# Products with zeros moved between three places in an attention and soft-MoE kernel

## The chip, the cores and the metric

The kernel runs on one core of a Trainium2 chip. The metric is device time in microseconds of one execution; several executions are taken and their median is compared. TensorE is called PE, VectorE DVE, ScalarE ACT, GpSimd POOL, and SyncE, which issues the stores, SP.

## The reference

The first part is attention over 4 batches, 8 heads, 768 positions and head size 64. Some heads see all earlier positions, the others only 4 first positions and a window of 64. The second part is a soft mixture of experts over the 3072 rows of the result (512 columns): 8 experts with 4 slots each.

```
scores = where(mask, q @ k.T / 8, -1e9);  a = softmax(scores);  x = a @ v      # as 3072 x 512
logits = x @ phi                                  # 3072 x 32
slot_input = softmax(logits, over rows).T @ x     # 32 x 512
h = relu(slot_input[e] @ w1[e]);  slot_out[e] = h @ w2[e]      # each expert e, w1 512x1024, w2 1024x512
out = softmax(logits, over slots) @ slot_out      # 3072 x 512
```

## The kernel before, in words

The work is a list of named operations. A planner (`Plan.run`) places them by keys, costs and free buffers, and so fixes one order; the program is then emitted in this order, and each engine works through its own queue.

Attention goes in sixteen groups, `p` from 0 to 15 (batch times pair of heads). In each, PE forms scores (L641) into a score bank (`scb`, two of them, two halves each), ACT takes exponentials (L713), DVE masks them (L658), PE multiplies them with the values into `pvb` (L773), DVE normalizes (L787), PE transposes the result (`XT.p`, L799) and DVE copies it (`XE.p`).

At the end of each batch come the products with phi (`LG.b`, L814), their exponentials (`EL.b`, L829, on ACT), the slots' sums (`DS.b`, L844), their addition on DVE (`SA.b`, L862 for the last batch) and a transpose of the exponentials (`TE.b`, L872). `LG.3` and `DS.3` are those of the last batch. Then `SI` (L929) folds the four partial sums with four small products, and a copy gives `siT`.

The experts follow. `H.e4.c` (L945) is the first layer for four experts at a time and one half of the hidden columns, 16 products each; ACT applies the ReLU, `TH` (L967) transposes, DVE copies. `W2.e` (L990) is the second layer of expert `e`, eight products into `pvb[:, 0, :]`. The last expert comes in two parts: `W2.7` gives columns 0 to 255, `W2.8` the rest. Between `W2.5` and `W2.6` stands `RW` (L1027), 24 products for the rows' sums. ACT scales the first half of the slots' output (`SOa`, L1004) after `W2.7` and the second half (`SOb`) after `W2.8`.

The output is formed from 30 products `OM.gi.r.d0` (L1056): six over columns 0 to 255 ahead of `W2.8`, six over columns 256 to 511, and 18 over all 512. `OM.0.0.0` is the first. ACT and DVE scale each into the output tile (L1064, L1066), and SP stores it in eleven pieces (L1083).

All weights come by DMAs issued by POOL (L283) in one fixed order; those of the last expert come last, in two pieces for `W2.7` and `W2.8`.

Apart from the work there are products of a tile of zeros (`zeros_for`, L1155 to L1158), whose results nobody reads. The dictionary `before` maps an operation's name to how many of them stand ahead of it and in which bank they write. One loop fills it from the planned order: in the first 22 us of the plan, and from the last product of attention to the last expert wherever the plan leaves PE a gap of 0.6 us or more, at most three each (none ahead of `W2`). After that loop, some entries are set by hand (L1150 to L1153), and these lines are what the change touches. The last loop emits the zeros and then the operation.

Of the kernel before, what the change touches and what calls it, by code (L numbers as in the profile page):

```python
# [173 lines left out]
def kernel(  # L174
# [19 lines left out]
    NE, DM, F = moe_w1.shape  # L194
# [52 lines left out]
    scb = [ps.tile([P, 2, 512], F32, name=f"sc{i}") for i in range(2)]  # L247
    trb = [ps.tile([P, 512], F32, name=f"tr{i}") for i in range(2)]
    pvb = ps.tile([P, 2, 512], F32, name="pv")
# [773 lines left out]
    cs = Buf("SC")  # L1023
# [83 lines left out]
    before, free, shift, hist = {}, 1.2, 0.0, []  # L1107
# [39 lines left out]
        before[o.name] = (min(max(0, int(us / (w / 2400))), 0 if o.name[:2] == "W2" else 3), 0, bank, c0)  # L1147


    for k in ("XT.15", "LG.3", "DS.3"):  # L1150
        del before[k]
    before[f"W2.{NE - 1}"] = (8, 0, pvb[:, 1, :], 0)
    before["OM.0.0.0"] = (2, 0, pvb[:, 1, :], 0)  # L1153

    def zeros_for(n, m, bank, c0):  # L1155
        for w in [512 - c0] * n + [128] * m:
# [43 lines left out]
```

## Time and profile before

| | |
|---|---|
| median of 3 runs | 150.12 us (148.64 to 151.61) |
| the profiled execution | 149.16 us, its span 147.4 us |
| PE busy | 124.9 us, 85% of the span |
| DVE busy | 111.5 us, 76% |
| ACT busy | 109.7 us, 74% |
| mean granted clock of PE | 0.961 |
| DMA | 33.03 MB, mean 224 GB/s |

Times in the profile are microseconds from the first instruction. Lines such as L990 are lines of the kernel. A row of the timeline has the start, the time from the first start to the last end, the engine, the line, what is written from what, and the count; in brackets stands the idle time of the engine before it and what ended that. Durations of PE's products overlap, since they are pipelined. A row of stretches has the stretch, its length, the busy time and number of instructions of PE, its weight loads, DVE, ACT and POOL, then the clock granted to PE (1.00 is full), the busy share of the DMA engines and the GB/s that they moved.

### The profile page before, as it was taken

To read this page: it belongs to the slowest core of one execution; us is meant where nothing else is said; L and a number is where in the kernel's file an instruction comes from. 1 tells how busy PE (TensorE), PEld (TensorE's weight loads), DVE (VectorE), ACT (ScalarE), POOL (GpSimd) and SP (SyncE) were. 2 spreads that over 40 slices of the span, in tenths; PEclk is the share of its full clock that TensorE was granted. 3 is DMA by queue.
4 is the path that set the end of the run, shared out by engine and by line. 5 is a ranking of instruction groups with operands and counts; after the bars stand their busy time and mean duration, and the time that the engine had idled before them with its cause. 6 is when DMAs were issued, how large, how long until landed. Compare 5 with 4: busy or idle time off the path is not lost.

```text
span 147.4 us, 4968 instructions
## 1 busy us (share of the span) xinstructions
PE 124.9 (85%) x2169; PEld 80.3 (54%) x2169; DVE 111.5 (76%) x244; ACT 109.7 (74%) x143; POOL 24.0 (16%) x48
## 2 busy tenths in 40 slices
PE   6989999989899998999999999998748999789000
PEld 2355566668576675877576775765633457332000
DVE  3889299987999899899999999999848330179100
ACT  3374899989999999999998999999712620399200
POOL 6921111320111121101400111010700000100000
PEclk9999999999999999999999999999997899999955
DMA  4999999999999999999999999999999999879995
GB/s 97 186 213 217 223 210 210 213 212 226 213 209 210 215 222 216 218 218 197 214 217 229 216 213 213 216 216 213 213 218 218 213 213 188 117 240 389 409 422 249
DMA packets 9608, 33.03 MB, mean 224 GB/s; under 512 B 867, under 2 KB 4595, under 8 KB 7283
## 3 DMA queue, kind: packets, MB, share of 16 engines
q0 software_dynamic: 6912, 26.09, 88.5%
q1 hardware_dynamic: 2672, 6.62, 11.7%
q8 instruction: 17, 0.28, 0.7%
q14 instruction: 5, 0.04, 0.1%
q10 hardware_dynamic: 2, 0.00, 0.0%
HBM read 52.49 MB, written 6.29 MB: 399 GB/s over the span
## 4 chain that ended last, share of the span: by engine, by line
PE 34%; DVE 18%; DMA 17%; ACT 16%; issue 4%; POOL 4%; ACTq 1%; POOLq 0%
DMA slot<-in_v_dram 17%; ACT pt L713 9%; PE pv L773 8%; PE sc L641 6%; DVE pt L658 4%; DVE xv L787 4%; POOL slot L283 3%; ACT slot L1064 3%; PE tr L611 3%; PE pv L990 2%; PE tr L799 2%; DVE xT L278 2%; PE sc L945 2%; DVE qk L278 2%; PE tr L945 2%
## 5 line engine op out<-in xcount | busy, mean ns | idle before, releaser
L713 ACT ACTIVATE pt<-sc 128x1024 bf16<-128x1024 f32 x80 | 76.7, 1045 | 2.9 <-PE sc L641 2.5
L641 PE MATMUL sc<-qk 64*128 64x512 bf16 (+3 forms) x256 | 31.3, 308 | 2.6 <-ACT pt L713 1.8
L658 DVE TENSOR_TENSOR pt<-pt,msk 128x1024 bf16<-128x1024 bf16 (+1 forms) x48 | 29.9, 639 | 0.5 <-ACT pt L713 0.4
L773 PEld LDWEIGHTS <-pt 128*128 128x128 bf16 x640 | 23.4, 97 | 6.7 <-issue 5.6
L773 PE MATMUL pv<-vx,pt 128*128 128x65 bf16 x352 | 26.1, 193 | 0.1
L773 PE MATMUL pv<-vf,pt 128*128 128x65 bf16 x288 | 20.9, 194 | 0.0
L641 PEld LDWEIGHTS <-qk 64*128 64x128 bf16 x256 | 10.2, 93 | 11.6 <-issue 4.7
L611 PE MATMUL tr<-ident,slot 128*64 128x128 bf16 (+1 forms) x448 | 15.5, 219 | 0.5 <-DMA slot<-in_v_dram 0.5
L787 DVE TENSOR_TENSOR xv<-pv,rs 128x768 bf16<-128x768 f32 x16 | 15.3, 958 | 0.6
L611 PEld LDWEIGHTS <-slot 128*64 128x64 bf16 (+1 forms) x448 | 12.7, 110 | 3.6 <-issue 3.2
L283 POOL DMA_DIRECT2D slot<-in_moe_w_dram x15 | 8.1, 543 | 38.6 <-PE tr L611 10.0
L278 DVE COPY qk<-tr 128x768 bf16<-128x768 bf16 (+2 forms) x24 | 12.9, 551 | 1.0 <-PE tr L569 0.6
L278 DVE COPY xv<-tr 128x768 bf16<-128x768 bf16 (+2 forms) x20 | 8.4, 431 | 2.6 <-PE tr L569 2.6
L799 PE MATMUL tr<-ident,xv 128*128 128x128 bf16 x96 | 8.1, 220 | 2.2 <-DVE xv L787 1.9
L1157 PE MATMUL pv<-zero 128*128 128x512 bf16 x33 | 8.3, 380 | 0.6 <-ACT msk L1004 0.6
L278 DVE COPY xT<-tr 128x768 bf16<-128x768 bf16 x14 | 7.7, 554 | 1.0 <-PE tr L799 0.8
L799 PEld LDWEIGHTS <-xv 128*128 128x128 bf16 x96 | 5.7, 97 | 4.7 <-DVE xv L787 2.3
L676 PE MATMUL tr<-ident,xv 128*128 128x128 bf16 x96 | 7.9, 220 | 0.1
L278 DVE COPY vx<-tr 128x768 bf16<-128x768 bf16 x14 | 7.7, 550 | 0.2 <-PE tr L676 0.2
L692 DVE TENSOR_TENSOR vf<-vx,fm 128x528 bf16<-128x528 bf16 x16 | 6.9, 430 | 0.3
L676 PEld LDWEIGHTS <-xv 128*128 128x128 bf16 x96 | 5.7, 97 | 2.4 <-issue 1.7
L1004 ACT ACTIVATE msk<-pv,rcs 128x256 bf16<-128x256 f32 x2 | 0.9, 474 | 8.0 <-PE pv L990 8.0
(121 smaller groups left out, 166.5 us busy)
## 6 DMA issues: line engine op xcount, KB each, us to landing
slot<-in_moe_w_dram POOLq DMA_DIRECT2D x9, 1024.0 KB, 22.4
out_dram<-slot SPq DMA_DIRECT2D x4, 1024.0 KB, 7.1
slot<-in_q_dram POOLq DMA_DIRECT2D x3, 768.0 KB, 19.8
slot<-in_k_dram POOLq DMA_DIRECT2D x3, 768.0 KB, 14.4
slot<-in_moe_w_dram POOLq DMA_DIRECT2D x2, 896.0 KB, 22.7
slot<-in_v_dram POOLq DMA_DIRECT2D x2, 768.0 KB, 12.7
out_dram<-slot SPq DMA_DIRECT2D x6, 256.0 KB, 2.7
slot<-in_v_dram POOLq DMA_DIRECT2D x2, 512.0 KB, 24.6
```

The costliest lines, as they stand in the source:

```text
L278: nc.vector.tensor_copy(dst, src)
L283: emit=lambda o: nc.gpsimd.dma_start(dst(), src))
L611: nc.tensor.transpose(t[64 * i:64 * (i + 1), :, s, :], rv[:, i, 8 * c + s, :], ident[0:nr, 0:nr])
L641: nc.tensor.matmul(scb[sc.slot][:, i, c:c + 128 * nb], kk, qq.rearrange("p b c -> p (b c)"), start=True, stop=True)
L658: nc.vector.tensor_tensor(pw, pw, mw, op=ALU.mult)
L676: nc.tensor.transpose(t[:, 128 * j:128 * (j + 1)], vT[:, 6 * n + j, :], ident)
L692: nc.vector.tensor_tensor(vfs[VFb[p].slot], vv, fm[:, n], op=ALU.mult)
L713: nc.scalar.activation(pTs[PTb[b, n].slot][:, :, 512 * g:512 * (g + 1)], scb[sc.slot], ACT.Exp, scale=scale)
L773: nc.tensor.matmul(pvb[:, h, 65 * i:65 * (i + 1)], lt, rhs, start=(j == 0), stop=(j == i))
L787: nc.vector.tensor_tensor(xo, pvw[:, :, :, 0:64], r.rearrange("p i (j o) -> p i j o", o=1).to_broadcast([P, 2, 6, 64]), op=ALU.mult)
L799: nc.tensor.transpose(t[:, 128 * i:128 * (i + 1)], xv[:, i, 128 * n:128 * (n + 1)], ident)
L1157: nc.tensor.matmul(bank[:, c0:c0 + w], zero[:, 0:128], zero[:, 0:w], start=(c0 == 0), stop=True, skip_group_check=True)
```

## The change

The hand-set entries of `before` differ. Ahead of `OM.0.0.0` there were two products of zeros and are none. Ahead of `W2.7` there were eight and are seven. Ahead of `LG.3` there were none and are two; ahead of `DS.3` there were none, and now the number that the loop worked out stands again; ahead of `SI` there were none and is one, in the half score bank that `RW` does not use. `XT.15` has none, as before. Nothing else is changed, and the planned order of the other operations is the same.

```
-    for k in ("XT.15", "LG.3", "DS.3"):
-        del before[k]
-    before[f"W2.{NE - 1}"] = (8, 0, pvb[:, 1, :], 0)
-    before["OM.0.0.0"] = (2, 0, pvb[:, 1, :], 0)
+    before["LG.3"] = (2, *before["LG.3"][1:])
+    before["SI"] = (1, 0, scb[1 - cs.slot][:, 1, :], 0)
+    del before["XT.15"]
+    before[f"W2.{NE - 1}"] = (7, 0, pvb[:, 1, :], 0)
```

## The prediction

> **What bounds the kernel now.** I read the clock by stretches first, then the order of TensorE's work from the end of attention on, then when the weights land, then the DMA share while the outputs are stored.
>
> Mean granted clock and busy time by stretches of 3.41 us (columns: us, busy time and count of each engine, clock, DMA share, GB/s):
>
> ```profile
> 108.69:112.10 3.41, 1.80 (x25) 0.88 (x22) 1.41 (x3) 1.67 (x3) 0.00 (x0) 1.00 1.05 221
> 112.10:115.51 3.41, 3.22 (x32) 1.24 (x36) 3.39 (x2) 0.69 (x1) 0.00 (x0) 0.50 1.01 211
> 115.51:118.93 3.42, 3.27 (x52) 1.87 (x44) 0.84 (x2) 2.74 (x11) 0.00 (x0) 1.00 1.05 220
> 125.75:129.17 3.42, 2.61 (x24) 1.19 (x26) 0.84 (x2) 1.42 (x4) 0.40 (x1) 1.00 0.73 101
> 129.17:132.58 3.41, 2.71 (x21) 1.28 (x18) 2.61 (x7) 3.05 (x7) 0.00 (x0) 1.00 0.77 252
> 135.99:139.41 3.42, 0.26 (x2) 0.00 (x0) 1.02 (x2) 1.35 (x3) 0.00 (x0) 1.00 1.01 414
> 139.41:142.82 3.41, 0.00 (x0) 0.00 (x0) 0.00 (x0) 0.00 (x0) 0.00 (x0) 0.50 1.01 420
> ```
>
> The clock is halved in 112.10 to 115.51, just after the stretch in which PE was busy for only 1.80 us, and again from 139.41, eight such stretches later, just after one with 0.26 us. So I read it as a grid: a thin stretch is followed by a halved one. Stretches with 2.61 and 2.71 us kept the clock. The dividing line lies between 1.80 and 2.61 us, in this trace's measure.
>
> The order of the work around the change (start, duration, engine; in brackets the idle time before):
>
> ```profile
> 108.31 0.51 PE L799 MATMUL tr<-ident,xv 128*128 128x128 bf16 x6 [0.88 <-DVE xv L787]
> 109.47 0.31 PE L814 MATMUL tr<-phi,xT 128*128 128x32 bf16 x6 [0.65 <-DVE xT L278]
> 110.20 0.61 PE L844 MATMUL tr<-xv,elg 128*32 128x512 bf16 x6 [0.42 <-ACT elg L829]
> 111.60 0.30 PE L929 MATMUL tr<-sum,msk 128*128 128x32 bf16 x4 [0.34 <-DVE msk L862]
> 112.29 1.90 PE L945 MATMUL sc<-slot,msk 128*32 128x512 bf16 x16 [0.38 <-DVE msk L278]
> 113.97 2.67 PE L945 MATMUL tr<-slot,msk 128*32 128x512 bf16 x32
> 119.00 1.48 PE L990 MATMUL pv<-slot,xT 128*32 128x512 bf16 x24
> 120.31 0.60 PE L990 MATMUL pv<-qk,xT 128*32 128x512 bf16 x8
> 124.12 0.62 PE L990 MATMUL pv<-pt,xT 128*32 128x512 bf16 x8
> 124.67 1.90 PE L1157 MATMUL pv<-zero 128*128 128x512 bf16 x8
> 126.50 0.40 PE L990 MATMUL pv<-qk,xT 128*32 128x256 bf16 x8
> 127.48 0.59 PE L1157 MATMUL pv<-zero 128*128 128x512 bf16 x2 [0.58 <-ACT msk L1004]
> 127.91 0.27 PE L1056 MATMUL sc<-msk,expT 128*128 128x256 bf16 x1
> 128.74 0.27 PE L1056 MATMUL sc<-msk,expT 128*128 128x256 bf16 x1 [0.23 <-ACT slot L1064]
> 129.06 0.40 PE L990 MATMUL pv<-qk,xT 128*32 128x256 bf16 x8
> 130.04 0.27 PE L1056 MATMUL sc<-msk,expT 128*128 128x256 bf16 x1 [0.58 <-ACT msk L1004]
> ```
>
> L799, L814, L844 and L929 are XT.15, LG.3, DS.3 and SI; L945 is the experts' first layer (H), L990 the second (W2): 124.12 is W2.6, 126.50 is W2.7, 129.06 is W2.8. PE looks like the bound of this stretch. But W2.6, W2.7 and W2.8 also need their weights, and those rows say (an issue's start, then the time to landing):
>
> ```profile
> 104.05 0.53 POOL L283 DMA_DIRECT2D pt<-in_moe_w_dram  x1 [7.52 <-PE pv L773]
> pt<-in_moe_w_dram POOLq DMA_DIRECT2D x1, 1024.0 KB, 19.5
> 104.57 1.77 POOL L283 DMA_DIRECT2D qk<-in_moe_w_dram  x2
> L283 POOL DMA_DIRECT2D qk<-in_moe_w_dram x2: 883/888/894, 104.6 to 105.5; - x2
> DMA to landing us min/median/max: 21.6/22.5/23.4
> ```
>
> The weights of W2.6 land at 104.05 + 19.5 = 123.55, those of W2.7 at 104.57 + 21.6 = 126.2, those of W2.8 at 105.5 + 23.4 = 128.9. (Counted from the issue's end, the last would be 129.8, after its user's start at 129.06; so the start is the right zero.) W2.7 starts 0.3 us after its landing, W2.8 less than 0.2. So the weights' stream bounds the kernel up to W2.8, with PE close behind. The stream itself ran at a DMA share of 1.01 or more in the three stretches from 108.69 to 118.93; no earlier PE work can hurry it.
>
> From there the outputs' stores are the bound:
>
> ```profile
> 128.50:129.00 0.50, 0.27 (x3) 0.10 (x1) 0.50 (x2) 0.50 (x2) 0.00 (x0) 1.00 0.00 0
> 129.00:129.50 0.50, 0.47 (x10) 0.21 (x9) 0.50 (x2) 0.50 (x2) 0.00 (x0) 1.00 0.07 16
> 129.50:130.00 0.50, 0.00 (x0) 0.00 (x0) 0.16 (x1) 0.49 (x2) 0.00 (x0) 1.00 0.25 88
> 130.00:130.50 0.50, 0.46 (x5) 0.41 (x5) 0.04 (x1) 0.15 (x1) 0.00 (x0) 1.00 1.05 346
> 130.50:131.00 0.50, 0.37 (x4) 0.08 (x2) 0.50 (x2) 0.50 (x2) 0.00 (x0) 1.00 0.65 213
> 131.00:131.50 0.50, 0.50 (x4) 0.25 (x4) 0.50 (x2) 0.50 (x3) 0.00 (x0) 1.00 1.06 348
> 145.00:146.00 1.00, 0.00 (x0) 0.00 (x0) 0.00 (x0) 0.00 (x0) 0.00 (x0) 0.50 0.91 377
> ```
>
> The DMA engines are nearly idle from 128.50 to 130.00 and work without a real gap from 131.00 to 146. What the first stores bring forward into that hole comes off the end.
>
> **The change part by part.** The order of the real work is the same; only products with zeros come and go. From the groups of instructions (count, busy us, mean ns of one), with the two groups that empty the output banks, used below:
>
> ```profile
> L1157 PE MATMUL pv<-zero 128*128 128x512 bf16 x10 | 2.5, 380 | 0.6 <-ACT msk L1004 0.6
> L1064 ACT ACTIVATE slot<-tr,rrow 128x512 f32<-128x512 f32 x5 | 3.3, 730 | 0.0
> L1066 DVE TENSOR_SCALAR slot<-sc,rrow 128x512 f32<-128x512 f32 x4 | 2.7, 742 | 0.0
> ```
>
> The eight took 1.90 us and the last one's own duration is 0.38, so one costs (1.90 - 0.38) / 7 = 0.22 us of PE's queue at full clock, 0.43 at half clock.
>
> *Two removed ahead of OM.0.* Their row shows that they waited 0.58 us for ACT's scaling (SOa, L1004) and ran only after it: they did not fill the wait, they stood behind it. OM.0 started 0.43 us after the wait had ended. Without them it starts at 127.48, as the first product after the other scaling does at 130.04 with nothing between. Gain for the first half stores: **0.43 us**. Behind it, OM.4 (128.74, waiting for ACT's evacuation) comes to 128.31, and W2.8 can come only as far as its landing, 128.9: a gain of 0.1 at most for the second halves.
>
> *One fewer ahead of W2.7.* 0.22 us less in the queue; W2.7 goes from 126.50 to 126.28, just behind its landing at 126.2. Gain **0.2 us**, and no more, whatever comes before.
>
> *Five put back between attention and experts* (two ahead of LG.3, two ahead of DS.3, one ahead of SI; the diff states 2 and 1, and the change's title gives 2 for the rest). The work that hides them is PE's wait for others: 0.65, 0.42 and 0.34 us against 0.43, 0.43 and 0.22. At DS.3 it is level, within 0.02 us, since products queue while the ones before finish. Cost **0** at full clock. If the cover is gone, at half clock, they need 0.86, 0.86 and 0.43: late by 0.21 + 0.44 + 0.09 = 0.7 us. They write the score bank that no exponential uses any more, so I see no wait for them. Their bounds are thus 0 and 0.7; I take 0, by the clock of 1.00 in that stretch.
>
> What they buy: the stretch from 108.69 goes from 1.80 us busy to about 1.80 + 5 x 0.22 = 2.9, over the 2.61 that kept the clock. Then H runs at full clock. The halved products took (113.97 - 112.29) / 16 = 0.105 us each, the full ones in W2 (120.31 - 119.00) / 24 = 0.055. Over 3.41 us of halved clock, less the 0.19 before H starts, that is 3.22 x (1 - 0.055/0.105) = **1.5 us** that PE is earlier at H's end. But W2.6 can then start only at 123.6 (0.5 earlier), seven zeros end near 125.7, and W2.7 waits for 126.2. So of the 1.5 us nothing beyond the 0.2 above is left: it turns into waiting for weights.
>
> The Trainium skill, page "TensorE: Matmul & The Clock Gate", section "HAM oscillation — how this bites in real kernels", gives the rule that the clock falls after idle gaps of PE above some 3.4 us. Here the longest gap in the thin stretch is 0.65 us, and the clock fell; the trace differs from the rule. By the rule the five products would buy nothing; that is the second rival.
>
> *What the tail loses in clock.* The stretch 125.75 to 129.17 is busy for 2.61 us with zeros in it. Without the two (0.59, less overlap some 0.45) and with the others done by 125.7 (some 0.8 of it), it holds about 1.4 to 1.9 us, near the 1.80 that lost the clock. Then 129.17 to 132.58 is halved: W2.8 up to 0.2 longer, the first product after SOb 0.1 longer, three wide products 0.06 longer each (0.43 against 0.37, half of 0.73 to 0.74, at which two engines empty banks). Bounds 0 and 0.5; since the stores queue anyway, I take **0.2**, as a loss.
>
> *Sum.* First half stores 0.43 + 0.2 = 0.63 earlier. The second halves come hardly earlier, so the join of the two sets of stores may give 0.1 back. End: -0.63 + 0.1 + 0.2 = **-0.3 us**. The profiled execution took 149.16 us (span 147.4, 1.76 around it) and would take 148.85; it lies 0.96 below the median of the runs, 150.12, so I predict **149.8 us**.
>
> **The rivals.** *First, more of H's gain arrives.* If the landings vary between executions and the weights of W2.7 come a microsecond sooner, W2.7 starts near 125.8: 0.7 earlier, and with 0.43 the first stores 1.1. Less the join, -1.0: 149.1 us. For it: the weights of W2.6 were 0.57 early. Against it: W2.8 was within 0.2 of its landing.
>
> *Second, the five do not raise the clock* (the rule above, or the grid lying otherwise). H stays as it is, W2.7 still comes to 126.28, the tail keeps more zeros in its stretch and its clock: -0.63 + 0.1 = -0.5, so 149.6 us. If the clock is already halved where the five stand, their 0.7 goes on top: 150.3 us.
>
> *Third, slower: the clock falls in the tail and counts in full.* Place: from 129.17, for want of the zeros between 125.75 and 129.17. Price: 0.2 + 0.1, and 0.06 for each of ten wide products if the halving holds for two stretches, 0.9 us with none of it hidden by queued stores. It decides from 0.5 us on, where it eats what the removed zeros saved; at 0.9 the end moves by -0.53 + 0.9 = +0.4: 150.5 us. For it: 1.80 us busy lost the clock earlier. Against it: the DMA engines have queued work from 131.00 to 146.
>
> **How the numbers follow.** Forecast 0.46; first rival 0.12; second 0.15, and 0.05 for its dearer form; third 0.20; 0.02 for anything else. All these lie within 1.0 us of the median, but three runs of before spread over 3 us (148.64 to 151.61), so the range gets 1.6 below and above: 148.2 to 151.4. Two per cent is 3.0 us, about what a measurement of this kernel can tell from no change. No case reaches it alone. Faster by over 2% needs the first rival and the spread: 0.06. Slower needs the third, lasting longer than I see reason for, or the dear form of the second, and the spread: 0.11. Within 2%: 0.83.
>
> **What would show it.** Right: five products of zeros in the gaps ahead of LG.3, DS.3 and SI with those three starting as before; clock 1.00 through H and H done some 1.5 us earlier; PE idle ahead of W2.6 or W2.7; OM.0 right behind SOa; W2.8 within 0.2 us of its landing; DMA idle time between 128.5 and 131 shorter by about half a microsecond. Wrong: H at half clock still; LG.3 or DS.3 late; W2.7 well ahead of 126 with the end following it; or a halved clock from W2.8 on with gaps in the stores' DMA share after 131.

## The result and the profile after

The kernel after takes 148.51 us (median of 20 runs, 148.19 to 149.11), the kernel before 148.95 us (20 runs, 148.57 to 151.61). The ratio is 0.9968, 95% interval 0.9952 to 0.9983: faster by 0.3%, clear of no change with this many runs, far below 2%. The three runs of before that stood ahead of the prediction had a median 1.2 us above that of the twenty.

The profiled execution of the kernel after took 148.61 us, span 146.8. Its order of work around the change (columns as before):

```profile
108.03 0.51 PE L799 MATMUL tr<-ident,xv 128*128 128x128 bf16 x6 [0.88 <-DVE xv L787]
108.37 0.59 PE L1157 MATMUL sc<-zero 128*128 128x512 bf16 x2
109.19 0.32 PE L814 MATMUL tr<-phi,xT 128*128 128x32 bf16 x6 [0.22 <-DVE xT L278]
109.35 0.59 PE L1157 MATMUL sc<-zero 128*128 128x512 bf16 x2
109.92 0.61 PE L844 MATMUL tr<-xv,elg 128*32 128x512 bf16 x6
110.81 0.38 PE L1157 MATMUL sc<-zero 128*128 128x512 bf16 x1
111.32 0.31 PE L929 MATMUL tr<-sum,msk 128*128 128x32 bf16 x4
112.01 1.05 PE L945 MATMUL sc<-slot,msk 128*32 128x512 bf16 x16 [0.38 <-DVE msk L278]
112.89 1.90 PE L945 MATMUL tr<-slot,msk 128*32 128x512 bf16 x32
117.14 1.48 PE L990 MATMUL pv<-slot,xT 128*32 128x512 bf16 x24
123.50 0.62 PE L990 MATMUL pv<-pt,xT 128*32 128x512 bf16 x8 [1.17 <-DMA pt<-in_moe_w_dram]
126.15 0.40 PE L990 MATMUL pv<-qk,xT 128*32 128x256 bf16 x8 [0.42 <-DMA qk<-in_moe_w_dram]
127.13 0.27 PE L1056 MATMUL sc<-msk,expT 128*128 128x256 bf16 x1 [0.57 <-ACT msk L1004]
128.82 0.40 PE L990 MATMUL pv<-qk,xT 128*32 128x256 bf16 x8 [0.47 <-DMA qk<-in_moe_w_dram]
```

The five products fill gaps and delay nothing: LG.3, DS.3 and SI each start 0.28 us earlier than before, as XT.15 ahead of them does. H's first 16 products take 1.05 us instead of 1.90, and the second layer behind H starts at 117.14 instead of 119.00: 1.86 us earlier, of which 0.28 stand ahead of H, so H gave the 1.5 us of the working. OM.0 starts as soon as SOa lets it. And the waits that the prediction looked for are there by name: W2.6, W2.7 and W2.8 now wait for DMAs.

When those weights land, from the issues and their times to landing:

```profile
103.77 0.53 POOL L283 DMA_DIRECT2D pt<-in_moe_w_dram  x1 [7.53 <-PE pv L773]
pt<-in_moe_w_dram POOLq DMA_DIRECT2D x1, 1024.0 KB, 19.7
L283 POOL DMA_DIRECT2D qk<-in_moe_w_dram x2: 881/888/894, 104.3 to 105.2; - x2
DMA to landing us min/median/max: 21.8/22.7/23.6
```

103.77 + 19.7 = 123.5, 104.3 + 21.8 = 126.1 and 105.2 + 23.6 = 128.8: the three starts, within 0.1 us.

The clock by stretches of its grid (cut some 0.16 us ahead of the clock's own edges, which lie at 129.88 and 133.29):

```profile
109.24:112.66 3.42, 2.91 (x37) 1.27 (x41) 1.68 (x3) 1.67 (x3) 0.00 (x0) 1.00 1.03 216
112.66:116.07 3.41, 3.41 (x64) 1.78 (x56) 2.72 (x2) 2.43 (x4) 0.00 (x0) 1.00 1.03 216
126.31:129.72 3.41, 1.64 (x22) 0.88 (x15) 1.33 (x3) 2.23 (x5) 0.40 (x1) 1.00 0.71 136
129.72:133.14 3.42, 3.35 (x12) 1.52 (x12) 2.30 (x5) 2.68 (x6) 0.00 (x0) 0.52 0.90 298
```

The stretch ahead of H is busy for 2.91 us and H keeps the full clock. The stretch with OM.0 in it holds 1.64 us, and the clock falls for the next one, while the output products run.

The DMA share at the stores:

```profile
129.00:129.50 0.50, 0.22 (x8) 0.10 (x1) 0.00 (x0) 0.23 (x1) 0.00 (x0) 1.00 0.86 276
131.00:131.50 0.50, 0.50 (x3) 0.22 (x3) 0.50 (x2) 0.48 (x2) 0.00 (x0) 0.50 0.98 334
131.50:132.00 0.50, 0.50 (x3) 0.20 (x2) 0.20 (x1) 0.35 (x1) 0.00 (x0) 0.50 0.40 135
```

The stores start in earnest at 129.0 instead of 130.0. But at 131.5 they run dry for 0.3 us: I read this as the first halves being out while the second halves, behind W2.8, are not there yet.

### The profile page after: what moved, and what is told of

It is laid out like the page before. It is cut to its first block, busy times and chain, and to the rows that moved or that the text cites. A ratio compares the mean times of both kernels' runs of the same rounds, so it can differ in the third digit from the quotient of the medians.

```text
span 146.8 us, 4972 instructions
## 1 busy us (share of the span) xinstructions
PE 125.4 (85%) x2171; PEld 80.9 (55%) x2171; DVE 111.6 (76%) x244; ACT 110.3 (75%) x143; POOL 24.0 (16%) x48
## 4 chain that ended last, share of the span: by engine, by line
DMA 33%; PE 23%; DVE 15%; ACT 14%; POOL 4%; issue 4%; ACTq 0%; POOLq 0%
DMA slot<-in_v_dram 17%; DMA qk<-in_moe_w_dram 16%; ACT pt L713 9%; PE pv L773 7%; PE sc L641 6%; DVE pt L658 4%; DVE xv L787 3%; POOL slot L283 3%; PE tr L611 3%; DVE qk L278 2%; ACT slot L1064 2%; PE tr L799 2%; DVE xT L278 2%; PE tr L676 2%; PE sc L1056 1%
## 5 line engine op out<-in xcount | busy, mean ns | idle before, releaser
L799 PEld LDWEIGHTS <-xv 128*128 128x128 bf16 x96 | 5.7, 97 | 4.7 <-DVE xv L787 2.2
L1066 DVE TENSOR_SCALAR slot<-tr,rrow 128x256 f32<-128x256 f32 (+1 forms) x6 | 3.3, 571 | 6.5 <-PE tr L1056 6.4
L1157 PE MATMUL pv<-zero 128*128 128x512 bf16 x30 | 7.5, 382 | 0.0
```

Of the source, the lines that this page charges most:

```text
L799: nc.tensor.transpose(t[:, 128 * i:128 * (i + 1)], xv[:, i, 128 * n:128 * (n + 1)], ident)
L1157: nc.tensor.matmul(bank[:, c0:c0 + w], zero[:, 0:128], zero[:, 0:w], start=(c0 == 0), stop=True, skip_group_check=True)
```

## The experiments

At first, the theory was that of the prediction: the end follows the landing of the weights, and the gain is the two products that stood behind SOa. The rival was that the gain is H at full clock. The ratios are those of the record with their 95% intervals; they are not the quotients of the medians.

**The two products ahead of OM.0 alone.**

```
-    before["OM.0.0.0"] = (2, 0, pvb[:, 1, :], 0)
```

> One part alone: only the two products of zeros ahead of OM.0 are taken out; eight ahead of W2.7, none ahead of LG.3, DS.3 and SI. First theory (the weights' landing sets W2.7 and W2.8, and the gain is the two products that stood behind SOa): OM.0 starts right after SOa, first stores 0.43 us earlier, the clock may fall in the tail for 0 to 0.5 us of that; H at half clock as before. 0.2 to 0.45 us faster than before, ratio 0.997 to 0.999. Rival (the gain is H at full clock, by the five products): no difference, ratio 1.000, or slower for the tail's clock, 1.002.

Measured: 149.08 us against 149.24, ratio 1.0001 (0.9969 to 1.0033). A gain of 0.3% is just inside the interval, one of 0.2% well so, so a small gain is not excluded, but nothing shows. Its profiled execution, one of the longer ones (150.2 us), shows what the prediction had missed. The stretches:

```profile
107.70:111.11 3.41, 1.70 (x24) 1.00 (x24) 1.36 (x3) 0.87 (x2) 0.00 (x0) 1.00 1.01 214
111.12:114.53 3.41, 2.73 (x31) 1.08 (x32) 3.00 (x3) 1.05 (x2) 0.00 (x0) 0.50 1.04 216
114.53:117.94 3.41, 3.41 (x40) 1.25 (x36) 1.18 (x2) 1.37 (x3) 0.00 (x0) 0.50 1.00 209
```

the order of work:

```profile
114.01 3.63 PE L945 MATMUL tr<-slot,msk 128*32 128x512 bf16 x32
127.71 0.40 PE L990 MATMUL pv<-qk,xT 128*32 128x256 bf16 x8
128.69 0.27 PE L1056 MATMUL sc<-msk,expT 128*128 128x256 bf16 x1 [0.58 <-ACT msk L1004]
129.84 0.40 PE L990 MATMUL pv<-qk,xT 128*32 128x256 bf16 x8
```

and the issue and landing of the last expert's weights:

```profile
104.59 1.77 POOL L283 DMA_DIRECT2D qk<-in_moe_w_dram  x2
DMA to landing us min/median/max: 21.5/22.4/23.2
```

Here the clock falls 1.0 us earlier than in before (111.12 against 112.12), and two stretches in a row are halved, both over H. H's middle 32 products take 3.63 us instead of 2.67. PE comes to W2.7 at 127.71, 1.6 us after its weights landed (104.59 + 21.5 = 126.1), and to W2.8 at 129.84. In such an execution PE is the bound, not the weights.

How often: the runs of the kernel before fall in two groups by mean granted clock, 0.956 or less and 0.958 or more. On this chip 18 of 35 are in the lower group (median 149.48 us) and 17 in the higher (148.73). The profiled execution of before, with one halved stretch ahead of the end, had 0.961, this one with two 0.955. On the chips of the later comparisons the groups are 11 runs with 149.22 and 6 with 148.6, 17 with 149.65 and 13 with 149.38, and 7 with 149.96 and 4 with 149.02. So the lower clock goes with a longer time on each chip, by 0.3 to 0.9 us. That it stands for a second halved stretch is read from a few traces, not shown for each run: the mean clock also counts the end, where PE has no more work and the clock fell at 139.43 in before, at 141.84 here.

**The five products alone.**

```
-    for k in ("XT.15", "LG.3", "DS.3"):
-        del before[k]
+    before["LG.3"] = (2, *before["LG.3"][1:])
+    before["SI"] = (1, 0, scb[1 - cs.slot][:, 1, :], 0)
+    del before["XT.15"]
```

> The other part alone: the five products ahead of LG.3, DS.3 and SI are put in; eight ahead of W2.7 and two ahead of OM.0 as before. First theory: H at full clock, PE some 1.5 us earlier at its end, and all but 0.2 us of this lost again in waits for the weights of W2.6 and W2.7; 0 to 0.2 us faster, ratio 0.9985 to 1.000. Rival: the whole gain of the change, 0.4 us, ratio 0.997.

Measured: 148.51 us against 149.24, ratio 0.9958 (0.9936 to 0.9979), all runs between 148.33 and 148.79 and with a mean clock of 0.969 or more. The rival is right: this part alone is the whole gain of the change, as far as the intervals tell, and the spread shrinks with it. Its tail kept the clock in the profiled execution:

```profile
129.72:133.14 3.42, 3.29 (x16) 1.28 (x15) 3.20 (x7) 3.31 (x7) 0.00 (x0) 1.00 1.03 343
```

**Both kernels without the last loads.** The same edit was made in before and after:

```
-  emit=lambda o: nc.gpsimd.dma_start(dst(), src))
+  emit=None if name in ("w14", "w15a", "w15b") else lambda o: nc.gpsimd.dma_start(dst(), src))
   ...
-  m = late_mem[i]() if i in late_mem else slots[wbuf[i].slot][:, :]
+  m = late_mem[min(i, 13)]() if i in late_mem else slots[wbuf[i].slot][:, :]
```

> The kernel before, leaving out the loads of the last two experts' second-layer weights; W2.6, W2.7 and W2.8 read those of the expert before them. All products stay. First theory: PE was only just behind these landings, so without them it keeps its own pace, H at half clock: W2.7 near 126.5, 0 to 0.4 us faster than before. Rival (the landings bind before the change already): over 0.6 us faster.

> The kernel after the change, with the same loads left out. First theory: the 1.5 us or more that PE gains by H at full clock are no longer lost in waits for weights: W2.6 at about 122.3, W2.7 near 124.3, first stores some 2 us earlier; 1.7 to 2.5 us faster than the kernel before with the same loads left out. Rival (PE's lead is lost elsewhere, in ACT, DVE or the stores): the two differ by 0.4 to 0.6 us, as with the loads.

Measured: before without the loads 149.53 us, ratio to before with them 1.0019 (0.9989 to 1.0049); after without them 146.75 us, ratio 0.9845 (0.9809 to 0.9881). Taking the weights' wait away gives the kernel before nothing (0 to 0.4 us faster was expected): PE's own pace was its bound. The kernel after, at ratios of 0.9968 and 0.9935 with the loads (the second is from a comparison below), gains about one per cent. So the change is worth 149.53 - 146.75 = 2.8 us without the loads, above the 1.7 to 2.5 expected, and 0.4 to 0.9 with them; the rest is spent waiting for weights. The profiled execution of before without them, its stretches,

```profile
105.56:108.97 3.41, 1.88 (x54) 1.60 (x50) 2.13 (x4) 0.00 (x0) 0.00 (x0) 1.00 1.04 219
108.97:112.38 3.41, 2.57 (x25) 1.05 (x25) 1.20 (x3) 1.67 (x3) 0.00 (x0) 0.50 1.00 209
112.39:115.80 3.41, 3.41 (x36) 1.25 (x32) 3.29 (x2) 0.80 (x2) 0.00 (x0) 0.50 1.00 209
```

its W2.7,

```profile
126.52 0.40 PE L990 MATMUL pv<-xv,xT 128*32 128x256 bf16 x8
```

and of after without them, W2.6 and W2.7:

```profile
122.36 0.62 PE L990 MATMUL pv<-xv,xT 128*32 128x512 bf16 x8
124.53 0.40 PE L990 MATMUL pv<-xv,xT 128*32 128x256 bf16 x8
```

W2.7 comes 2.0 us earlier, close to what was expected (near 124.3). The execution of before without the loads also has two halved stretches in a row, with a mean clock of 0.950, and yet its W2.7 stands at 126.52, where the profiled execution of before has it with one. Its attention ended 0.7 us sooner (XT.15 at 107.61 against 108.31), and the first of the two stretches lies almost wholly ahead of H, which starts at 112.03. So two halved stretches need not make PE late for the weights: how far they do depends on where they lie over H and on when attention ends, and the mean clock tells neither.

**Zeros inside the waits.** Two kernels add products of zeros to the kernel after, where PE waits anyway: the first with the first entry below, the second with all three.

```
+    before["OM.0.0.0"] = (2, 0, scb[1 - cs.slot][:, 1, :], 0)
+    before[f"W2.{NE}"] = (2, 0, pvb[:, 1, :], 0)
+    before["OM.0.0.256"] = (2, 0, scb[1 - cs.slot][:, 1, :], 0)
```

> The kernel after the change, with two products of zeros ahead of OM.0 once more, but written into the free half of a score bank instead of the bank that SOa reads. First theory: they run inside PE's wait of 0.57 us for SOa and cost nothing, OM.0 starts as in the kernel after; with 0.45 us more work in the stretch the clock falls less often in the tail: 0 to 0.3 us faster than the kernel after, ratio to before 0.995 to 0.997. Rival (two more products cost 0.43 us wherever they write): the gain is gone, ratio 0.999 to 1.000.

> The kernel after the change, with two products of zeros in each of three waits of PE's tail: for SOa (0.57 us) and for SOb (0.57 us) into the free half of a score bank, and ahead of W2.8, while it waits for its weights (0.47 us), into the second half of the bank of W2, which nobody reads then. First theory: each pair, 0.43 us, fits its wait; the stretch ahead of the output products is then busy enough to keep the clock in every phase: 0.2 to 0.4 us faster than the kernel after, ratio to before 0.994 to 0.9955. Rival (the tail's clock costs nothing, since stores queue): as the kernel after, 0.997. Second rival (a pair stands in the way): 0.998 to 1.001.

Measured: 148.41 us, ratio 0.9948 (0.9925 to 0.9971), and 148.42 us, ratio 0.9957 (0.9932 to 0.9981), beside the five products alone at 148.51 on the same chip. All of their runs kept a mean clock of 0.969 or more. The zeros do run in the waits, as the first of the two shows behind W2.7 (126.41), where OM.0 comes 0.98 us after W2.7 with the zeros as it does without them (126.15 to 127.13):

```profile
126.75 0.60 PE L1157 MATMUL sc<-zero 128*128 128x512 bf16 x2
127.39 0.27 PE L1056 MATMUL sc<-msk,expT 128*128 128x256 bf16 x1
```

But neither is told apart from the other kernels with the five. A second comparison on one chip puts three kernels side by side:

> The kernel after the change, once more, as the base of the three beside it. New theory (the five products' worth is that H never runs at half clock, for one stretch or for two; the missing two ahead of OM.0 give 0.43 us to the first stores and take some of it back where the tail's clock falls): its executions fall in two groups by mean clock, 0.98 and 0.96, about 0.3 to 0.4 us apart; ratio to before 0.995 to 0.997.

> The kernel after the change with the two products ahead of OM.0 put back as before, behind SOa in the bank that SOa reads. New theory: the tail's clock holds in nearly every execution (mean clock 0.97 or more), OM.0 comes 0.43 us later; both nearly cancel, 0.0 to 0.2 us slower than the kernel after, with a narrower spread. First theory, as predicted: 0.2 to 0.4 us slower than the kernel after.

> The kernel after the change with those two products in the free half of a score bank, inside the wait for SOa. New theory: OM.0 as early as in the kernel after and the tail's clock held: 0.1 to 0.3 us faster than both its neighbours. Rival (the queue of stores hides the start of OM.0 and the tail's clock alike): the three lie within 0.1 us.

The second of these three adds `before["OM.0.0.0"] = (2, 0, pvb[:, 1, :], 0)` to the kernel after, the third the same with the score bank. Measured, against 149.48 us for before: 148.60 (0.9935, 0.9911 to 0.9960), 148.61 (0.9947, 0.9917 to 0.9977) and 148.54 (0.9930, 0.9902 to 0.9959). The three medians lie within 0.1 us, as the rival said; with intervals of some 0.4 us to each side, a difference of 0.2 us would not show. The spread of the second was not narrower (148.31 to 149.45 against 148.19 to 149.17), against what was expected. The runs of the kernel after spread from 0.960 to 0.981 in mean clock but do not fall in two groups as expected. The half microsecond at OM.0 is in the traces all the same. The kernel after, OM.0 and W2.8 in the timeline and then the stretch in which the stores pause:

```profile
127.08 0.27 PE L1056 MATMUL sc<-msk,expT 128*128 128x256 bf16 x1 [0.57 <-ACT msk L1004]
128.76 0.40 PE L990 MATMUL pv<-qk,xT 128*32 128x256 bf16 x8 [0.46 <-DMA qk<-in_moe_w_dram]
```

```profile
131.50:132.00 0.50, 0.50 (x4) 0.19 (x2) 0.50 (x1) 0.50 (x2) 0.00 (x0) 1.00 0.76 244
```

With two products behind the wait for SOa, the same:

```profile
127.32 0.59 PE L1157 MATMUL pv<-zero 128*128 128x512 bf16 x2 [0.57 <-ACT msk L1004]
127.75 0.27 PE L1056 MATMUL sc<-msk,expT 128*128 128x256 bf16 x1
128.98 0.40 PE L990 MATMUL pv<-qk,xT 128*32 128x256 bf16 x8
```

```profile
131.50:132.00 0.50, 0.50 (x4) 0.19 (x2) 0.50 (x2) 0.50 (x2) 0.00 (x0) 1.00 1.03 338
```

Without the two, W2.8 waits for its weights and the stores pause at 131.5, with the clock at 1.00 this time, so the pause is not the clock's. With them, W2.8 follows OM.5 directly and the stores do not pause. By the medians, the early start is given back before the end. That it is the wait for weights that opens the pause is not shown by these traces: with OM.0 alone, W2.8 came 1.1 us after its weights had landed, and the stores paused all the same, for some 0.4 us, most of it here:

```profile
132.00:132.50 0.50, 0.50 (x4) 0.24 (x3) 0.50 (x3) 0.50 (x2) 0.00 (x0) 1.00 0.38 129
```

**Is it given back for want of weights?** The five products alone and the kernel after, both with the last loads left out:

> The kernel before with the five products put in (eight ahead of W2.7, two behind SOa ahead of OM.0), leaving out the loads of the last two experts' second-layer weights; W2.6, W2.7 and W2.8 read those of the expert before them. Theory: with the loads the 0.43 us of the two products are lost because the second halves cannot follow the first (W2.8 waits for its weights, and the stores run dry between the two sets). Without the loads W2.8 follows, and this kernel is 0.4 to 0.65 us slower than the kernel after with the same loads left out (0.43 for the two, 0.22 for the eighth, less what the tail's clock gives back). Rival (the start of OM.0 never matters): within 0.15 us of it.

> The kernel after the change with the same loads left out, once more, as the base of the one beside it: W2.7 near 124.5, W2.8 right behind OM.5; 2.3 to 2.8 us faster than the kernel before with its loads.

Measured: 147.69 us (six runs, 147.10 to 148.75) and 146.99 (146.69 to 147.13), ratios to before 0.9880 (0.9832 to 0.9929) and 0.9821 (0.9778 to 0.9864). The medians are 0.70 us apart, a little over the 0.4 to 0.65 expected. The intervals of the ratios overlap, but five of the first six runs lie above all of the other six. The traces agree, by the distance that PE needs. W2.6 and W2.8 of the five alone,

```profile
121.83 0.62 PE L990 MATMUL pv<-xv,xT 128*32 128x512 bf16 x8
126.77 0.40 PE L990 MATMUL pv<-xv,xT 128*32 128x256 bf16 x8
```

and of the kernel after:

```profile
122.45 0.61 PE L990 MATMUL pv<-xv,xT 128*32 128x512 bf16 x8
126.75 0.40 PE L990 MATMUL pv<-xv,xT 128*32 128x256 bf16 x8
```

From W2.6 to W2.8 it is 4.94 us with the three products and 4.30 without: 0.64, the 0.43 and 0.22 of the working. (These two executions themselves took the same time, 147.10 and 147.07 us, since the first came to W2.6 0.62 us sooner.) Without the wait for weights, the removal of the three counts, by the medians.

**Three of the five.**

```
-    before["LG.3"] = (2, *before["LG.3"][1:])
+    del before["LG.3"]
```

> The kernel after the change without the two products ahead of LG.3; three of the five stay. If the busy time of the whole stretch decides, it loses 0.43 of some 1.1 us: H falls to half clock in some phases, mean clock under 0.96 in some executions, and 0.1 to 0.4 us slower than the kernel after. Rival (what stands nearest to H is enough): as the kernel after, within 0.1 us.

Measured: 148.73 us, ratio 0.9940 (0.9915 to 0.9966), beside 148.60 for the kernel after. By time the two are not told apart. By clock three of its twelve runs are under 0.96, as expected of some, against none of the twelve beside them; but the twenty of the first result have one too (0.954), so this is a hint. Its profiled execution:

```profile
105.39:108.80 3.41, 1.88 (x49) 1.46 (x45) 1.92 (x4) 0.06 (x1) 0.17 (x1) 1.00 1.04 219
108.80:112.21 3.41, 3.03 (x23) 1.26 (x25) 1.23 (x3) 1.61 (x3) 0.00 (x0) 0.50 1.04 216
112.21:115.63 3.42, 3.42 (x64) 1.41 (x56) 3.26 (x2) 2.06 (x3) 0.00 (x0) 1.00 1.00 208
```

The clock falls at 108.80, but the halved stretch, with the three products of zeros near H in it, is busy enough, and H has the full clock again but for its first 0.2 us. In this execution the clock falls once more at 129.28, as in the kernel after, so its low mean clock does not mean that H ran slowly.

## Why the prediction was right or wrong

**Right in number, and by luck.** The end moved by about what was forecast: -0.3 us predicted, -0.44 measured (0.25 to 0.71 by the interval), and the time lies in the range. But the sum gave all of its gain to the removed products (0.63) and none to the five that were put in, and the runs show the reverse: the five alone bring the whole gain (ratio 0.9958), the two ahead of OM.0 alone none that shows (1.0001). Two wrong terms made up for each other.

**Right in mechanism.** The five products stood inside gaps, LG.3, DS.3 and SI lost nothing, H ran at full clock and was done 1.5 us earlier, PE then waited for weights, OM.0 came directly behind SOa, and the stretch with OM.0 lost its clock. The second rival, in the form that the five do not raise the clock, is refuted, and so is the third (slower). One sign that was named for being wrong did come: a halved clock behind W2.8 with a gap in the stores' DMA share after 131. In another execution of the same kernel the gap is there at full clock. The first rival (more of H's gain arrives) came nearest, but for another reason than it gave: not that the weights land sooner, but that PE is often later.

**Wrong: the term of the five products, and the path behind it.** The prediction says that the weights' stream bounds the kernel before up to W2.8, with PE close behind, and so gave the five "nothing beyond the 0.2". It read this from one execution, in which W2.7 stood 0.3 us behind its landing and no row of W2.6, W2.7 or W2.8 waits for a DMA. The runs show that PE's pace was the bound: without those loads the kernel before is no faster (1.0019), and the five, which only hurry PE, are worth 0.73 us of 149.24 by the medians. In the runs of before with the higher mean clock the forecast of 0.2 would do (148.73 against 148.51 with the five); in those with the lower, about half of them, it is 0.97. There a second stretch seems to be halved. Where both lie over H, as in the trace with OM.0 alone, PE reaches W2.7 some 1.6 us after the landing and W2.8 about 1 us after. How many of the slower runs are of this kind stays open. I priced the grid lying otherwise only as a cost of the added products (0.7 us), not as a loss of the kernel before. The 0.2 of one fewer ahead of W2.7 goes the same way: with the five in place and all eight still there, W2.7 waits 0.21 us for its weights.

**Wrong: the term of the two products ahead of OM.0.** The 0.43 us at OM.0 was right. For the join of first and second halves I took 0.1 back. The stores' pause between 131.0 and 132.0 (0.3 and 0.2 us in two executions of the kernel after) and the comparison of three kernels within 0.1 us put it nearer to the whole 0.43 while the weights of W2.8 bind. It reappears without the loads (0.70 us, with the eighth product).

**Wrong: what can be told apart.** I took 2% as what a measurement of this kernel can tell from no change. Twenty runs on each side give an interval of 0.3%, and the gain lies clear of no change. And the level, 149.8, rested on a median of three runs that two long ones had lifted.

**Open.** Why the two products ahead of OM.0 gain nothing in the runs of before in which PE is late: by the account above their 0.43 us should count there, but with OM.0 alone the five runs of the lower clock have a median of 149.43, against 149.48 for before. And what the fall of the clock at 129.88 costs: the kernels with zeros in the waits were at most 0.1 us faster by their medians than those beside them, less than the runs can show. None of the variants beats the kernel after by more than its interval.

## What to carry to other kernels

One profiled execution shows one position of the clock's grid, the row of 3.41 us stretches. Before a loss is called hidden, move the grid by hand through the thin places and ask what the worst position costs, since a filler's worth may lie in the executions that were not profiled.

An earlier start of the first part of an output is worth something only if the second part can follow it; look for what releases the second. And a filler that must wait for the same event as the work behind it fills nothing: write it to a bank that the awaited instruction does not read.

## What the runs showed of the hardware

The clock's edges lie on a grid of 3.41 us. In the traces they are whole multiples of it apart, as 112.12, 115.53 and 139.43 in before, or 108.80, 112.21, 129.28, 132.69 and 139.51 with three of the five. The grid lies elsewhere in each execution: the edge near the end of attention is at 112.12 in before, 111.12 with OM.0 alone, 108.97 in before without the last loads.

How busy PE was in a stretch, by the trace's own measure, does not give a sharp border for the fall. Cut at the clock's own edges, stretches at full clock with 1.56, 1.70, 1.78 and 1.88 us of PE were followed by a halved one (in after, with OM.0 alone, in before, and in before without the last loads). But these two, with OM.0 alone and with two products behind the wait, were followed by one at full clock, and so were all with 1.94 us or more:

```profile
135.01:138.42 3.41, 1.88 (x7) 0.48 (x5) 2.78 (x5) 3.10 (x6) 0.00 (x0) 1.00 1.05 415
134.37:137.78 3.41, 1.72 (x6) 0.45 (x5) 2.56 (x4) 2.88 (x5) 0.00 (x0) 1.00 1.04 424
```

So between 1.7 and 1.9 us both were seen, and what else decides there is not known. At half clock more was needed to get out: 2.57 and 2.73 us did not lift the clock, 2.87 and 3.03 (with three of the five) did.

The Trainium skill, page "TensorE: Matmul & The Clock Gate", section "What's actually happening", says that the window is 3413 ns long and free-running, not started by the kernel; these traces agree in both. They do not agree with the rule about idle gaps quoted in the prediction: with 1.88 us busy of 3.41, so with no gap over 1.53, the clock fell.
